# First stage of an attention and two-MLP kernel: exponentials kept unnormalized, rows of values with their sums, normalized on DVE and turned on TensorE

## The chip, the cores and the metric

The kernel runs on one core of one Trainium2 chip. The metric is the device time of one execution in microseconds; three executions were timed before the change. Five engines work side by side, each through its own queue in order: TensorE (PE in the profile, its weight loads PEld), VectorE (DVE), ScalarE (ACT), GpSimd (POOL) and SyncE (SP, which issues DMAs).

## The reference

```
# q, k, v: (2, 8, 768, 64); n_global = 8, n_local = 96
scores = (q @ k^T) / sqrt(64) + bias          # ALiBi: -slope[h] * distance
keep   = (key < n_global) | (0 <= query - key < n_local)
scores = where(keep, scores, -1e9)
a = exp(scores - max)
a = a / (sum(a) + 1e-9)
x = a @ v                                     # 1536 x 512 over both batches
h = elu(x @ w_in);  y = h @ w_out             # 512 -> 2048 -> 512
out = max(y @ w1, y @ w2, y @ w3) @ w_out2    # 512 -> 768 -> 512
```

The weights and inputs are float32 values, the weights passed as 64-bit words that the kernel converts itself.

## The kernel before

Attention is cut into 48 steps: six groups `g` of 256 queries, four pairs of heads `hp`, two blocks `t` of 128 queries. A step takes one block of 128 queries for two heads (`u` = 0, 1). Its keys are a window of 232 columns (96 earlier, 8 global, 128 own); the first block of a batch has only its own 128. I call these wide and narrow steps. In the first group (steps 0 to 7) steps alternate narrow and wide; steps 8 to 15 are wide.

One step runs through these functions: `scores_pe` (two matmuls into PSUM), `scores_dve` (one DVE instruction for each head adds the bias and takes the minimum), `scores_act` (an exponential for each head with the row sum accumulated, which is read out by an instruction of its own), `sums` (ACT adds 1e-9 to the two sums), `recip` and `norm` (DVE: reciprocal, then one multiplication for each head), `turn_pe` (PE turns the probabilities: four transposes of 116 keys, two for a narrow step), `turn_act` (ACT copies the turned tile from PSUM to SBUF), `values_pe` (the values are the stationary operand, the turned probabilities stream past; the result is already turned, head dimension on partitions), `values_high` (ACT rounds it into `xh`) and `values_low` (DVE writes the rest into `xl`).

The first stage is the loop in `windowed`, 18 iterations written out by hand, each engine's order being the order of the calls. Iteration k works on four steps at once: scores, exponentials and sums of step k, normalizing of k-1, turning of k-2, values of k-3. Steps 0 to 15 (the first 512 rows of `x`) are finished there, and steps 16 and 17 begun. The turned tiles cycle through three PSUM banks. From iteration 7 each iteration also takes a piece of the conversion of three weight chunks (`words`), on DVE (`c_low`, `c_word`, `c_rest`) or ACT (`c_rebase`, `c_high`). SP issues the loads in the order of the calls: values (`load_values`, one tile for two steps, each partition 2 KB), queries and keys (`load_pair`), weights (`w_load`). POOL scales the queries (`scale_queries`).

The stage ends with the product `h` of the first weight chunk with `x`: its first half in iterations 16 and 17, the second half at the start of `run`, which goes on with three blocks of 512 rows through the first MLP, the other 32 attention steps between them, and then the second MLP. `run` uses `scores_act`, `norm`, `turn_pe` and `values_pe` in its own order.

Of the kernel before, what the change touches and what calls it, by code (L numbers as in the profile page):

```python
# [12 lines left out]
F32 = mybir.dt.float32  # L13
# [5 lines left out]
ALU = mybir.AluOpType  # L19
PSUM = bass.MemoryType.PSUM  # L20

B, H, S, D = 2, 8, 768, 64
DM, FF, FF2 = 512, 2048, 768
NT = B * S
P = 128
# [9 lines left out]
CH = WIN // 2  # L35
BIG = 1e30
KW = 2 * P + WIN - P + G
GRP = 2 * P
BLOCKS = [512, 512, 512]
# [8 lines left out]
def numbers(nc, pool, n_ap):  # L48

    ni = pool.tile([P, 4], I32, name="ni")  # L50
    nc.sync.dma_start(ni, n_ap.bitcast(I32).partition_broadcast(P))
    w = pool.tile([P, 4], F32, name="nw")
    nc.vector.tensor_copy(w, ni)
    w2 = w.rearrange("p (a b) -> p a b", b=2)
    hi = pool.tile([P, 2], F32, name="nhi")
    nc.vector.scalar_tensor_tensor(
        hi, w2[:, :, 0], 0.0, w2[:, :, 1], op0=ALU.is_lt, op1=ALU.add
    )
    nf = pool.tile([P, 2], F32, name="nf")
    nc.vector.scalar_tensor_tensor(  # L60
        nf, hi, 4294967296.0, w2[:, :, 0], op0=ALU.mult, op1=ALU.add
    )
    return nf[:, 0:1], nf[:, 1:2]


def covered(nc, pool, ng, nl, flag):

    f = pool.tile([P, 4], F32, name="nok")
    nc.vector.tensor_scalar(f[:, 0:1], ng, 0.0, None, op0=ALU.is_ge)
    nc.vector.tensor_scalar(f[:, 1:2], ng, float(G), None, op0=ALU.is_le)  # L70
    nc.vector.tensor_scalar(f[:, 2:3], nl, 1.0, None, op0=ALU.is_ge)
    nc.vector.tensor_scalar(f[:, 3:4], nl, float(PREV + 1), None, op0=ALU.is_le)
    ok = pool.tile([P, 1], F32, name="ok")
    nc.vector.tensor_reduce(ok, f, axis=AX.X, op=ALU.min)
    nc.vector.tensor_copy(flag, ok)
# [33 lines left out]
class Windowed:  # L109
# [4 lines left out]
    def __init__(self, tc, ctx, io, ps, xy, wt, act):  # L114
        self.nc, self.io, self.ps, self.xy, self.wt, self.act = tc.nc, io, ps, xy, wt, act
        self.const = ctx.enter_context(tc.tile_pool(name="acst", bufs=1))
        self.qk = ctx.enter_context(tc.tile_pool(name="qk", bufs=2))
        self.sm = ctx.enter_context(tc.tile_pool(name="sm", bufs=3))
        self.steps = [
            (g, hp, t) for g in range(NT // GRP) for hp in range(HP) for t in range(2)  # L120
        ]
        self.loaded, self.scaled = 0, set()
        self.qk_t, self.v_t = {}, {}
        self.s_t, self.p_t, self.t_t, self.at_t = {}, {}, {}, {}
        self.xraw = {}

    def positions(self, scratch):

# [62 lines left out]
    def load_values(self, k, early=False):  # L191

        if k >= len(self.steps) or k % 2:
            return
        p = k // 2
        pool, tag = (self.act, "gl") if early and p % 2 else (self.qk, "v")
        v = pool.tile([P, 2, 2, P], F32, tag=tag, name="v")
        self.nc.sync.dma_start(
            v.rearrange("p t c f -> p (t c f)"), self.io["v2"][p]
        )  # L200
        self.v_t[k], self.v_t[k + 1] = v[:, 0], v[:, 1]

    def scores_pe(self, k, tags=("S0", "S1"), m=1):
# [50 lines left out]
            m = self.p_t[k][1]  # L254
            self.nc.vector.reciprocal(m[:, 6:8], m[:, 4:6])

    def scores_act(self, k):
        if k >= len(self.steps):
            return
        n = self.geom(k)[-1]  # L260
        p, m = self.p_t[k]
        for u in range(2):
            o = slice(u * WIN, u * WIN + n)
            self.nc.scalar.activation(  # L264
                p[:, o], p[:, o], AF.Exp, bias=m[:, u:u + 1], scale=-1.0,
                accum_out=m[:, 2 + u:3 + u],
            )

    def norm(self, k):
# [37 lines left out]
    def values_pe(self, k, x=None):  # L307
# [5 lines left out]
        for c in range(nch):  # L313
            for u in range(2):
# [3 lines left out]
                    start=c == 0, stop=c == nch - 1,  # L318
                )

    def values_high(self, k, x):

        if k >= 0:
            g, hp, t = self.steps[k]
            o = g * GRP + t * P
            self.nc.scalar.copy(x[0][:, hp, o:o + P], self.t_t[k][0][:, 0:P])

    def values_low(self, k, x):
        if k >= 0:
            g, hp, t = self.steps[k]  # L330
            o = g * GRP + t * P
            self.nc.vector.tensor_tensor(
                x[1][:, hp, o:o + P], self.t_t.pop(k)[0][:, 0:P],
                x[0][:, hp, o:o + P].bitcast(F32), op=ALU.subtract,
            )

# [807 lines left out]
def windowed(tc, ctx, io, flag):  # L1144
    nc = tc.nc
    f = Feed(tc, ctx, io)
    own = ctx.enter_context(ExitStack())
    at = Windowed(tc, own, io, f.ps, f.xy, f.wt, f.act)
    at.close = own.close
    with tc.manual_schedule():  # L1150
        scratch = [f.cv.tile([P, 512], F32, tag="wr", name="sc") for _ in range(2)]
        at.load_pair(0, True)
        f.warm(WARM)
        at.positions(scratch)
        ng, nl = numbers(nc, at.const, io["nn"])
        for p in range(1, 3):
            at.load_pair(p, True)
        at.scale_queries(0)
        at.bases(ng, nl, 0, P + WIN)
        first = BLOCKS[0] // GRP * 8  # L1160
        x = f.split_tiles()

        def convert():
            f.c_rebase(0)
            f.c_low(0)
            yield
            f.c_word(0, 0)
            yield
            f.c_word(0, 1)
            yield  # L1170
            f.c_high(0)
            f.c_rebase(1)
            f.c_low(1)
            yield
            f.c_word(1, 0)
            yield
            f.c_rest(0)
            yield
            f.c_word(1, 1)
            yield  # L1180
            f.c_high(1)
            f.c_rebase(2)
            f.c_low(2)
            yield
            f.c_rest(1)
            yield
            f.c_word(2, 0)
            yield
            f.c_word(2, 1)
            yield  # L1190

        words = convert()
        h = f.ps.tile([P, 512], F32, tag="h", name="h")
        for k in range(first + 2):
            e = k % 2
            at.load_values(k, True)
            if e == 0:
                at.load_pair(k // 2 + 3, k < first)
                at.scale_queries(k // 2 + 1)
            if k <= first:  # L1200
                at.scores_pe(k, (("S0", "S1"), ("y0", "y1"))[e], 1 + (k == first))
            if k >= first:
                f.product(h, f.w[0][:, 0], x, GRP, 0, (k - first) * 6, 6)
            at.values_pe(k - 3)
            at.turn_pe(k - 2, ("TX", "y2", "y3")[k % 3])
            if k < FILL[0]:
                f.fill(at.ident, FILL[1])
            at.scores_dve(k, True)
            at.values_high(k - 3, x)
            at.turn_act(k - 2, nc.scalar.copy)  # L1210
            at.scores_act(k)
            at.sums(k)
            at.recip(k - 1)
            at.norm(k - 1)
            at.values_low(k - 3, x)
            if k >= CONV:
                next(words, None)
            if k in WLOAD:
                f.w_load()
        at.values_pe(first - 1)  # L1220
        at.turn_pe(first, "TX")
        at.values_high(first - 1, x)
        at.turn_act(first, nc.scalar.copy)
        at.values_low(first - 1, x)
        at.recip(first + 1)
        at.norm(first + 1)
        next(words, None)
        f.run(at, first + 2, x, h, lambda: covered(nc, at.const, ng, nl, flag))
# [104 lines left out]
```

## Time and profile before

| what | value |
|---|---|
| median of three executions | 554.83 us (554.69 to 556.24) |
| the profiled execution | 554.8 us, its span 553.0 us |
| busy in the span: PE, DVE, ACT, POOL | 532.5, 394.5, 291.3, 105.1 us |
| mean granted TensorE clock | 0.996 of full speed |

The span goes from the first to the last instruction. Busy time adds up instructions of an engine, overlaps counted once; PE's includes the modelled drain of its passes. In a timeline row the first number is the start, the second the duration, both in us, then engine, line, operation, output and inputs, shapes and count; the brackets hold idle time before it and what ended it. One DVE or ACT instruction can begin a little before the one ahead of it has drained, so the time between two starts is what it costs the queue.

### The profile page before, as it was taken

To read this page: it belongs to the slowest core of one execution; us is meant where nothing else is said; L and a number is where in the kernel's file an instruction comes from. 1 tells how busy PE (TensorE), PEld (TensorE's weight loads), DVE (VectorE), ACT (ScalarE), POOL (GpSimd) and SP (SyncE) were. 2 spreads that over 40 slices of the span, in tenths; PEclk is the share of its full clock that TensorE was granted. 3 is DMA by queue.
4 is the path that set the end of the run, shared out by engine and by line. 5 is a ranking of instruction groups with operands and counts; after the bars stand their busy time and mean duration, and the time that the engine had idled before them with its cause. 6 is when DMAs were issued, how large, how long until landed. Compare 5 with 4: busy or idle time off the path is not lost.

```text
span 553.0 us, 7717 instructions
## 1 busy us (share of the span) xinstructions
PE 532.5 (96%) x2718; PEld 423.2 (77%) x2718; DVE 394.5 (71%) x811; ACT 291.3 (53%) x647; POOL 105.1 (19%) x105
## 2 busy tenths in 40 slices
PE   8889999999999999999999999999999999999995
PEld 6457777767777888887888878878888888888884
DVE  6998999999835444333366747687886979789873
ACT  5998777787846555555355555552147322324120
POOL 4200222222310000000000015431025410335000
PEclk9989999999999999999999999999999999999999
DMA  8919444442201111100000031313008500786024
GB/s 291 393 55 352 159 155 172 140 153 72 91 20 43 29 44 43 38 21 18 0 2 0 1 114 39 114 39 114 1 20 287 208 0 24 241 326 228 2 78 156
DMA packets 23454, 59.20 MB, mean 107 GB/s; under 512 B 2416, under 2 KB 2416, under 8 KB 23408
## 3 DMA queue, kind: packets, MB, share of 16 engines
q1 hardware_dynamic: 18368, 49.46, 25.6%
q10 hardware_dynamic: 5040, 9.18, 4.4%
q8 instruction: 23, 0.38, 0.3%
q14 instruction: 23, 0.19, 0.1%
HBM read 49.19 MB, written 9.44 MB: 106 GB/s over the span
## 4 chain that ended last, share of the span: by engine, by line
PE 72%; DVE 17%; ACT 9%; issue 1%; POOL 0%; ACTq 0%; DVEq 0%; POOLq 0%
PE h L662 19%; PE y L693 11%; DVE wr L457 8%; PE y L937 7%; PE y L701 5%; PE y L1031 4%; PE y L662 4%; PE S L937 4%; ACT w L465 3%; PE S L1031 2%; PE TX L937 2%; DVE p L243 2%; PE S L662 2%; PE TX L293 2%; ACT wr L446 2%; DVE e L687 2%
## 5 line engine op out<-in xcount | busy, mean ns | idle before, releaser
L662 PE MATMUL h<-xh,w 128*128 128x512 f32 (+1 forms) x432 | 115.7, 389 | 0.8 <-ACT xh L642 0.8
L499 POOL TENSOR_TENSOR w<-wr,w 128x512 fp32r<-128x512 f32 x42 | 62.8, 1506 | 232.6 <-ACT w L498 230.4
L693 PE MATMUL y<-gh,w 128*128 128x512 f32 x384 | 98.7, 399 | 0.6 <-ACT gh L669 0.6
L662 PEld LDWEIGHTS h<-xh,w 128*128 128x128 f32 x432 | 79.1, 188 | 19.5 <-issue 1.7
L693 PEld LDWEIGHTS y<-gh,w 128*128 128x128 f32 x384 | 69.6, 188 | 17.1 <-ACT gh L669 1.7
L687 DVE SCALAR_TENSOR_TENSOR e<-e,h 128x512 f32<-128x512 f32 x48 | 32.9, 686 | 54.9 <-ACT e L683 54.9
L662 PE MATMUL h<-xl,w 128*128 128x512 f32 (+1 forms) x216 | 65.9, 386 | 0.0
L498 ACT CAST w<-wr 128x512 fp32r<-128x512 f32 x42 | 27.6, 663 | 63.5 <-DVE wr L489 51.1
L264 ACT ACTIVATE p<-p,m 128x232 f32<-128x232 f32 (+1 forms) x96 | 44.8, 470 | 21.3 <-DVE m L243 21.3
L682 ACT ACTIVATE e<-h 128x512 f32<-128x512 f32 x48 | 28.6, 596 | 50.4 <-PE h L662 45.8
L701 PE MATMUL y<-gl,w 128*128 128x512 f32 x192 | 51.6, 390 | 0.0
L457 DVE SCALAR_TENSOR_TENSOR wr<-wr 128x1024 uint32<-128x1024 uint32 (+1 forms) x36 | 49.9, 1396 | 0.7
L489 DVE SCALAR_TENSOR_TENSOR wr<-wr 128x512 uint32<-128x512 uint32 x48 | 44.2, 922 | 7.5 <-ACT wr L481 6.0
L662 PEld LDWEIGHTS h<-xl,w 128*128 128x128 f32 x216 | 40.3, 188 | 8.3
L669 ACT CAST gh<-e 128x512 fp32r<-128x512 f32 x48 | 29.8, 621 | 30.1 <-DVE e L687 30.1
L937 PE MATMUL y<-t,w 128*128 128x512 f32 x180 | 42.7, 389 | 0.0
L701 PEld LDWEIGHTS y<-gl,w 128*128 128x128 f32 x192 | 36.0, 188 | 8.0 <-issue 0.3
L674 POOL TENSOR_TENSOR gl<-e,gh 128x512 fp32r<-128x512 f32 x16 | 21.0, 1313 | 102.8 <-ACT gh L669 102.8
L937 PEld LDWEIGHTS y<-t,w 128*128 128x128 f32 x180 | 33.8, 188 | 7.0
L674 DVE TENSOR_TENSOR gl<-e,gh 128x512 fp32r<-128x512 f32 x32 | 22.1, 692 | 19.9 <-ACT gh L669 19.9
L187 POOL TENSOR_SCALAR raw<-raw,qsc 128x256 f32<-128x256 f32 x24 | 18.5, 770 | 78.6 <-DMA raw<-qk 78.5
L683 ACT ACTIVATE e<-e 128x512 f32<-128x512 f32 x48 | 30.4, 633 | 1.5
(155 smaller groups left out, 841.9 us busy)
## 6 DMA issues: line engine op xcount, KB each, us to landing
wr<-wa SPq DMA_DIRECT2D x14, 1024.0 KB, 7.1
wr<-wb SPq DMA_DIRECT2D x24, 512.0 KB, 4.5
v<-v SPq DMA_DIRECT2D x24, 256.0 KB, 2.7
part<-row ACTq DMA_DIRECT2D x24, 256.0 KB, 4.2
raw<-qk SPq DMA_DIRECT2D x16, 312.0 KB, 3.8
row<-part SPq DMA_DIRECT2D x12, 256.0 KB, 3.2
out<-rows ACTq DMA_DIRECT2D x11, 256.0 KB, 2.5
raw<-qk SPq DMA_DIRECT2D x8, 260.0 KB, 3.4
```

The lines of the kernel that those rows point to most:

```text
L264: self.nc.scalar.activation(p[:, o], p[:, o], AF.Exp, bias=m[:, u:u + 1], scale=-1.0, accum_out=m[:, 2 + u:3 + u],)
L457: self.nc.vector.scalar_tensor_tensor(r[..., 0], r[..., 1], v, r[..., 0], op0=op, op1=ALU.bitwise_or)
L489: self.nc.vector.scalar_tensor_tensor(t, a, c, t, op0=op, op1=ALU.bitwise_or)
L499: nc.gpsimd.tensor_tensor(w[:, u, 1], v, w[:, u, 0].bitcast(F32), op=ALU.subtract)
L662: nc.tensor.matmul(out[:, o:n], w[:, part % 2, c * P:c * P + P], (xl if part == 2 else xh)[:, c, o:n], start=c == 0 and part == 0, stop=c ...
L674: (engine or self.nc.vector).tensor_tensor(gl[:, 0:n], e[:, 0:n], gh[:, 0:n].bitcast(F32), op=ALU.subtract)
L683: self.nc.scalar.activation(e, e, AF.Exp, scale=-1.0)
L687: self.nc.vector.scalar_tensor_tensor(e, e, -1.0, h, op0=ALU.add, op1=ALU.max)
L693: self.nc.tensor.matmul(y[e][:, 0:n], w[:, a, e * P:e * P + P], g[0][:, 0:n], start=fc == 0 and a == 0, stop=False,)
L701: self.nc.tensor.matmul(y[e][:, 0:n], w[:, 0, e * P:e * P + P], g[1][:, 0:n], start=False, stop=fc == NFC - 1,)
L937: self.nc.tensor.matmul(out, w[:, u, i % 2, b + c * P:b + c * P + P], o[:, i // 2, c], start=c == i == 0, stop=c == 1 and i == 2,)
L1031: nc.tensor.matmul(o, t[:, a, r], w[:, u, b], start=u == k == 0, stop=u == 1 and k == 2,)
```

## The change

In the first stage the exponentials stay unnormalized. `load_values` leaves a column of ones at each end of the 128 value columns (a memset on POOL, and a load in pieces of 512 bytes). `scores_act` drops the accumulated sum for steps below 16. `turn_pe` and `turn_act` come one iteration earlier, on step k-1. `values_rows`, on step k-2, takes the turned exponentials as the stationary operand and streams 65 columns (64 values and the ones) for each head, so that the result has queries on partitions and each head's sum in a column. `rows_norm` (DVE, step k-2) adds 1e-9 to the sums, takes reciprocals and multiplies the rows. `rows_turn` (PE, step k-3) turns the 128x128 result, and `values_high` and `values_low` read it from there. Steps 16 and 17 keep the old way.

```diff
@@ load_values
-        v = pool.tile([P, 2, 2, P], F32, tag=tag, name="v")
-        self.nc.sync.dma_start(
-            v.rearrange("p t c f -> p (t c f)"), self.io["v2"][p]
-        )
+        if k < self.rows:
+            v = pool.tile([P, 2, 2, P + 2], F32, tag=tag, name="v")
+            w = v.rearrange("p t c f -> p (t c) f")
+            self.nc.gpsimd.memset(w[:, :, 0:P + 2:P + 1], 1.0)
+            self.nc.sync.dma_start(
+                w[:, :, 1:P + 1], self.io["v2"][p].rearrange("p (a f) -> p a f", f=P)
+            )
+        else:
...
@@ scores_act
-                accum_out=m[:, 2 + u:3 + u],
+                accum_out=m[:, 2 + u:3 + u] if total else None,
@@ new functions
+    def values_rows(self, k):
...
+        at, v, x = self.at_t.pop(k), self.v_t.pop(k), self.t_t[k][0]
+        kk, nch = (CH, 2) if self.geom(k)[0] else (P, 1)
+        for u in range(2):
+            o = slice(u * (D + 1), (u + 1) * (D + 1))
+            for c in range(nch):
+                a = (nch * u + c) * P
+                self.nc.tensor.matmul(
+                    x[:, o], at[0:kk, a:a + P], v[0:kk, c, o], start=c == 0, stop=c == nch - 1
+                )
+    def rows_norm(self, k):
...
+        nc, x = self.nc, self.t_t[k][0]
+        m = self.sm.tile([P, 8], F32, tag="m", name="r", bufs=4)
+        y = self.y_t[k] = self.sm.tile([P, P], F32, tag="yn", name="yn", bufs=2)
+        nc.vector.tensor_scalar(
+            m[:, 0:2], x[:, 0:2 * D + 2:2 * D + 1], 1e-9, None, op0=ALU.add
+        )
+        nc.vector.reciprocal(m[:, 2:4], m[:, 0:2])
+        nc.vector.tensor_tensor(
+            y.rearrange("p (u d) -> p u d", u=2),
+            x[:, 1:1 + 2 * D].rearrange("p (u d) -> p u d", u=2),
+            m[:, 2:4].unsqueeze(2).to_broadcast([P, 2, D]), op=ALU.mult,
+        )
+    def rows_turn(self, k):
+        if k >= 0:
+            self.nc.tensor.transpose(
+                self.t_t[k][0][:, 2 * P:3 * P], self.y_t.pop(k), self.ident
+            )
@@ loop in windowed
                 at.scores_pe(k, (("S0", "S1"), ("y0", "y1"))[e], 1 + (k == first))
+            at.rows_turn(k - 3)
             if k >= first:
                 f.product(h, f.w[0][:, 0], x, GRP, 0, (k - first) * 6, 6)
-            at.values_pe(k - 3)
-            at.turn_pe(k - 2, ("TX", "y2", "y3")[k % 3])
+            if k <= first:
+                at.turn_pe(k - 1, ("TX", "y2", "y3")[k % 3])
+            at.values_rows(k - 2)
             if k < FILL[0]:
                 f.fill(at.ident, FILL[1])
             at.scores_dve(k, True)
             at.values_high(k - 3, x)
-            at.turn_act(k - 2, nc.scalar.copy)
-            at.scores_act(k)
-            at.sums(k)
-            at.recip(k - 1)
-            at.norm(k - 1)
+            if k <= first:
+                at.turn_act(k - 1, nc.scalar.copy)
+            at.scores_act(k, k >= first)
+            if k >= first:
+                at.sums(k)
             at.values_low(k - 3, x)
+            at.rows_norm(k - 2)
+            if k > first:
+                at.recip(k - 1)
+                at.norm(k - 1)
...
-        at.values_pe(first - 1)
+        at.rows_turn(first - 1)
         at.turn_pe(first, "TX")
```

## Rows read from the trace of the kernel before

**Rows 1.** The page's chain that ended last: shares of the span by engine.
```profile
PE 72%; DVE 17%; ACT 9%; issue 1%; POOL 0%; ACTq 0%; DVEq 0%; POOLq 0%
```

**Rows 2.** Two windows: length; PE, PEld, DVE, ACT, POOL busy (instructions); clock; DMA share; GB/s.
```profile
20.00:25.00 5.00, 3.80 (x34) 2.35 (x36) 4.93 (x15) 4.52 (x17) 0.51 (x2) 1.00 1.04 392
...
30.00:35.00 5.00, 4.92 (x36) 2.97 (x32) 4.93 (x19) 3.73 (x15) 0.00 (x0) 0.72 0.33 116
```

**Rows 3.** Timeline of ACT in one wide step without a conversion.
```profile
34.29 0.49 ACT L264 ACTIVATE p<-p,m 128x232 f32<-128x232 f32 x1
...
34.69 0.19 ACT L264 ACTIVATION_READ_ACCUMULATOR p<-p,m 128x1 f32 x1
34.78 0.47 ACT L264 ACTIVATE p<-p,m 128x232 f32<-128x232 f32 x1
...
35.49 0.25 ACT L326 CAST xh<-y 128x128 fp32r<-128x128 f32 x1
...
35.73 0.59 ACT L304 COPY p<-y 116x512 f32<-116x512 f32 x1
...
36.21 0.49 ACT L264 ACTIVATE p<-p,m 128x232 f32<-128x232 f32 x1
```

**Rows 4.** Timeline: first exponentials of steps 3, 7, 10, 11, 17; the stage's end.
```profile
11.48 0.49 ACT L264 ACTIVATE p<-p,m 128x232 f32<-128x232 f32 x1
...
18.10 0.49 ACT L264 ACTIVATE p<-p,m 128x232 f32<-128x232 f32 x1
...
25.18 0.49 ACT L264 ACTIVATE p<-p,m 128x232 f32<-128x232 f32 x1 [0.54 <-DVE m L243]
...
29.07 0.52 ACT L264 ACTIVATE p<-p,m 128x232 f32<-128x232 f32 x1
...
44.19 0.49 ACT L264 ACTIVATE p<-p,m 128x232 f32<-128x232 f32 x1 [0.16 <-DVE m L243]
...
47.19 0.60 ACT L682 ACTIVATE e<-h 128x512 f32<-128x512 f32 x1 [0.86 <-PE h L662]
```

**Rows 5.** Timeline of DVE in one step with a conversion.
```profile
20.94 1.23 DVE L457 SCALAR_TENSOR_TENSOR wr<-wr 128x1024 uint32<-128x1024 uint32 x1
...
22.07 0.38 DVE L243 CUSTOM_DVE_ANT_0 p<-y,rel 128x232 f32<-128x232 f32 x1
...
22.71 0.15 DVE L255 RECIPROCAL m<-m 128x2 f32<-128x2 f32 x1
...
22.90 0.59 DVE L277 TENSOR_SCALAR p<-p,m 128x232 f32<-128x232 f32 x2
...
23.41 0.29 DVE L332 TENSOR_TENSOR xl<-y,xh 128x128 fp32r<-128x128 f32 x1
...
23.61 1.22 DVE L457 SCALAR_TENSOR_TENSOR wr<-wr 128x1024 uint32<-128x1024 uint32 x1
```

**Rows 6.** Timeline of PE: three and four turning passes, values passes, passes of `h`.
```profile
13.62 0.54 PE L293 MATMUL y<-ident,p 128*116 128x128 f32 x3
13.62 0.65 PE L293 MATMUL y<-ident,p 128*116 128x128 f32 x4
...
36.36 0.66 PE L316 MATMUL y<-p,v 116*64 116x128 f32 x8
...
38.52 0.97 PE L662 MATMUL h<-xh,w 128*128 128x256 f32 x6
```

**Rows 7.** Groups of DVE instructions, 18 to 47.2 us: busy us, mean ns | idle before.
```profile
L332 DVE TENSOR_TENSOR xl<-y,xh 128x128 fp32r<-128x128 f32 x8 | 2.3, 285 | 1.2 <-ACT xh L326 1.2
...
L243 DVE DVE_READ_ACCUMULATOR2_ANT m<- 128x1 f32 x20 | 1.6, 82 | 0.0
```

**Rows 8.** Timeline of loads and POOL: first values issued; queries scaled.
```profile
2.60 0.43 SPq L198 DMA_DIRECT2D v<-v  x1
...
4.02 0.49 POOL L187 TENSOR_SCALAR raw<-raw,qsc 128x256 f32<-128x256 f32 x1
...
13.85 0.48 POOL L187 TENSOR_SCALAR raw<-raw,qsc 128x256 f32<-128x256 f32 x1 [3.51 <-DMA raw<-qk]
```

More of the change, by code (lines that the diff above doesn't have):

```diff
@@ L124, in __init__ @@
         self.s_t, self.p_t, self.t_t, self.at_t = {}, {}, {}, {}
-        self.xraw = {}
+        self.xraw, self.y_t = {}, {}
     def positions(self, scratch):
@@ L196, in load_values @@
         pool, tag = (self.act, "gl") if early and p % 2 else (self.qk, "v")
-        v = pool.tile([P, 2, 2, P], F32, tag=tag, name="v")
-        self.nc.sync.dma_start(
-            v.rearrange("p t c f -> p (t c f)"), self.io["v2"][p]
-        )
+        if k < self.rows:
[6 more added lines that the diff above has]
+        else:
+            v = pool.tile([P, 2, 2, P], F32, tag=tag, name="v")
+            self.nc.sync.dma_start(
+                v.rearrange("p t c f -> p (t c f)"), self.io["v2"][p]
+            )
         self.v_t[k], self.v_t[k + 1] = v[:, 0], v[:, 1]
@@ L255, in recip, with scores_act @@
             self.nc.vector.reciprocal(m[:, 6:8], m[:, 4:6])
-    def scores_act(self, k):
+    def scores_act(self, k, total=True):
         if k >= len(self.steps):
@@ L319, in values_pe @@
                 )
+    def values_rows(self, k):
+        if k < 0:
+            return
+        at, v, x = self.at_t.pop(k), self.v_t.pop(k), self.t_t[k][0]
[8 more added lines that the diff above has]
+    def rows_norm(self, k):
+        if k < 0:
+            return
+        nc, x = self.nc, self.t_t[k][0]
[14 more added lines that the diff above has]
+                self.t_t[k][0][:, 2 * P:3 * P], self.y_t.pop(k), self.ident
+            )
     def values_high(self, k, x):
@@ L325, in values_high @@
             o = g * GRP + t * P
-            self.nc.scalar.copy(x[0][:, hp, o:o + P], self.t_t[k][0][:, 0:P])
+            self.nc.scalar.copy(x[0][:, hp, o:o + P], self.t_t[k][0][:, 2 * P:3 * P])
     def values_low(self, k, x):
@@ L332, in values_low @@
             self.nc.vector.tensor_tensor(
-                x[1][:, hp, o:o + P], self.t_t.pop(k)[0][:, 0:P],
+                x[1][:, hp, o:o + P], self.t_t.pop(k)[0][:, 2 * P:3 * P],
                 x[0][:, hp, o:o + P].bitcast(F32), op=ALU.subtract,
@@ L1159, in windowed @@
         at.bases(ng, nl, 0, P + WIN)
-        first = BLOCKS[0] // GRP * 8
+        first = at.rows = BLOCKS[0] // GRP * 8
         x = f.split_tiles()
```

## The prediction, made before the changed kernel was run

> **What bounds the kernel now.** The chain of work that ended last gives TensorE (PE) most of the span, then DVE and ACT [rows 1]. That share is an average over stages. The change touches one stage, the 18 iterations of the loop in `windowed`, so I read that stage next: its windows, then its timeline. In the windows DVE and ACT are busy up to 4.9 of 5 us, while PE falls to 3.8 [rows 2]; PE's busy time also holds the drain of each pass, so PE is not the bound here.
>
> The timeline shows two kinds of step (I date a step by the start of its first exponential). A step without a weight conversion is ACT's: exponential, read of its sum, exponential, read and `sums`, copy to `xh`, copy of the turned tile, next exponential, back to back, 34.29 to 36.21 = 1.92 us [rows 3]. A step with a conversion on DVE is DVE's: conversion 1.13 (20.94 to 22.07), score passes 0.64, reciprocal 0.19, two normalizing passes 0.51, `xl` 0.20, next conversion at 23.61: 2.67 us [rows 5]. The first eight steps alternate narrow and wide tiles and have no conversion before step 7; steps 3 to 7 take 18.10 - 11.48 = 6.62, or 3.31 a pair [rows 4]. Steps 10 and 14 convert on ACT and are the longest: 25.18 to 29.07, 3.89 us [rows 4]. The stage ends when the product `h` reaches ACT at 47.19, where ACT had stood idle 0.86 [rows 4]; what the stage gains or loses there goes on to the end one for one.
>
> **What the change takes away.** On ACT the read between the exponentials goes (34.69 to 34.78, 0.09), and so do the second read and `sums`: the second exponential, begun at 34.78, needs 0.40 like the first, and the next work began at 35.49, so 0.31. That is 0.40 of 1.92 [rows 3]. On DVE reciprocal and normalizing go, 0.19 + 0.51 = 0.70 [rows 5].
>
> **What it adds on DVE.** `rows_norm` is three instructions, each waiting for the one before: a sum of 128x2, a reciprocal of 128x2, a product of 128x128. The reciprocal today holds its successor for 0.19 [rows 5]; the sum has its shape, so 0.19 each. The product has the shape and the PSUM source of `xl`, 0.285 long [rows 7], of which the queue is held 0.20 [rows 5]. So DVE pays 0.58 for 0.70, and the result is there after 0.19 + 0.19 + 0.29 = 0.67. No row shows a two-column read from PSUM or a scale repeated along a row. Bounds for the 0.67: two instructions as short as DVE's shortest, 0.08, and the product make 0.45 [rows 7]; three as long as a normalizing pass, 0.59 / 2, make 0.89 [rows 5]. I take 0.67, from the nearest shapes.
>
> **What it adds on PE.** Today the values are the weights, 64 columns wide, and the four matmuls of the code show as eight passes in 0.66 us [rows 6]. Afterwards the turned exponentials are the weights, 128 columns wide, and 65 columns of values stream past. The rows bound the spacing of these passes: as today, (0.66 - 0.27) / 7, near 0.055; as in the product `h`, 128-column weights with 256 streamed columns, six in 0.97, near 0.135; the turning passes, 116-column weights with 128 streamed columns, end 0.11 apart (0.54 to 0.65) [rows 6]. What grows is the weights, so I take 0.11. A last pass of 0.27, less half of 0.11 for half the columns, is 0.22: the rows are out after 7 x 0.11 + 0.22 = 0.99. The bounds are 0.6 and 1.17.
>
> [...]
>
> `rows_turn` is one turning pass more, 0.11.
>
> **The order closes a new loop.** PE works in order: scores of k, `rows_turn(k-3)`, `turn_pe(k-1)`, `values_rows(k-2)`. The `rows_turn(k-2)` that follows in the next iteration waits for DVE's `rows_norm(k-2)`, which waits for this iteration's last PE work. Queued behind the waiting `rows_turn` are the next turn and through it ACT's copy and next exponential; only the scores go ahead of it. Before, nothing went from PE to DVE and back within one step. A handover costs about 0.05 (a copy of 0.59 from 35.73 ends at 36.32, the values follow at 36.36) [rows 3, 6]. One wide turn of the loop: four turning passes 0.44, rows 0.99, handover, DVE 0.67, handover, `rows_turn` 0.11 = 2.31, against 1.92. A narrow tile has half the passes: turning a narrow one and making rows of a wide one takes 0.22 + 0.99 + 0.88 = 2.09, the reverse 0.44 + 0.55 + 0.88 = 1.87. A pair is 3.96, against 3.31.
>
> **The sum.** *Up to step 7:* two pairs, 2 x 0.65 = 1.3. Ahead of them the turn and copy of step k-1 now stand between its exponentials and those of k, some 0.6 us where nothing waits at first; part of it is caught up on the narrow steps, and step 3 starts 0.2 late. Together +1.5.
> *Steps 7 to 17.* To step 11: steps 7 and 8 about even, step 9 DVE's with 2.67 - 0.12, step 10 ACT's with -0.40: -0.5. From 11 to 14: `rows_norm` now stands behind `xl`, which waits for ACT's conversion; counted from that conversion's end, DVE reaches the next scores after 0.30 + 0.20 + 0.58 + 1.13 + 0.40 = 2.61, while step 11's exponential starts after 0.72 (`xh` 0.24, copy 0.48); so 1.89, then twice 2.55: 7.0, against 36.21 - 29.07 = 7.14 [rows 3, 4]: -0.1. From 14 to 17: step 14 takes 3.5; the first six passes of `h`, which ran under ACT's conversion at 38.52 [rows 6], are now queued behind the waiting `rows_turn` and ahead of the turn, 6 x 0.135: 1.89 + 0.8; then 2.55. That is 8.7 against 44.19 - 36.21 = 7.98 [rows 3, 4]: +0.7. Together +0.1.
> *The end:* iteration 17 has `rows_norm(15)` besides the old reciprocal and normalizing of step 16, ahead of the last conversion and `xl(15)`, for which `h` waits: +0.6.
> In all about +2.1 us. The profiled execution took 554.8 with its span of 553.0, and the median of the runs is 554.83, so the sum stands for both: 556.9.
>
> **Costed at nothing.** The memsets of the ones columns: POOL idles in this stage, 3.51 us before the tile scaled at 13.85 alone [rows 8]. The loads of values, in pieces of 512 bytes and each behind a memset in POOL's queue, are the third rival; without slack a late one would stop PE at `values_rows`.
>
> **Rivals.** *The loop is short, and the removed work shows* (faster). The place is `values_rows` with `rows_norm`: if together they take under 1.84 - 0.44 - 0.10 - 0.11 = 1.19 (I have 1.66; the lower bounds make 1.05), a wide step is set by exponentials, turn and copy, 0.40 + 0.47 + 0.05 + 0.38 + 0.05 + 0.48, about 1.84, and the first steps come out even. With the short `rows_norm` each of five DVE-bound steps saves 0.12 + 0.22, the two ACT steps 0.40 each, and the end is even: about -2.3, 552.5. For it speaks that the stretch from 30 to 35 us, where the granted clock was 0.72 [rows 2], could be spared as well. Against it: it takes both lower bounds. 12 in 100.
> *The loop costs what the removed work gives* (no change): passes at 0.09, or 0.55 on DVE, take 0.15 us off each of some ten steps: 555.4. 31 in 100.
> *Late values* (slower still). The first load of values was issued at 2.60, with POOL busy up to the queries scaled at 4.02 [rows 8]; behind a memset it goes some 2 us later, and the `raw` and weight loads behind it in SP's queue too. If small pieces halved the rate, eight loads of 0.64 us at some 400 GB/s [rows 2] would add 5 us to a full queue. Against it: the `raw` tile scaled at 13.85 [rows 8] is first used for step 10, whose exponential starts at 25.18 [rows 4]. Were the cover used up, 2 to 3 us more: 559.5. 5 in 100. [...]
> That the change does nothing would need the reads of the sums to stay; nothing speaks for it.
>
> **How the numbers follow.** A measurement of this kernel tells 0.3%, 1.7 us, from no change. The forecast by itself, 556.5 to 558.5, has 52 in 100; with late values slower has 0.57, same 0.31, faster 0.12. Both upper bounds add 0.4 to a wide turn and as much to a pair's halves, and 0.2 to each DVE-bound step: about +5.3, 560.1. The range starts at 553.9, which leaves out the faster rival, and ends at 560.1.
>
> **What would show it.** Right: in steps 3 to 7 PE waits for DVE at `rows_turn` and ACT for PE at the copy; pairs near 4 us; ACT's busy time in the stage falls by some 6 us; `h` reaches ACT near 49.3. Wrong: eight row passes well under 0.9 us, a `rows_norm` under 0.5, ACT without gaps in steps 3 to 7, or PE waiting for a load of values.

## The result and the profile after

The changed kernel takes 563.39 us (five runs, 563.2 to 564.59); the kernel before takes 555.81 beside it (five runs, 554.69 to 556.24). The ratio is 1.0146, with an interval of 1.0129 to 1.0163: slower by 1.5%, 7.6 us, where 2.1 were forecast. The profiled executions stand at 563.39 (span 561.6, granted clock 0.998) and 554.8 (span 553.0), so they lie 8.6 apart; what follows divides up these 8.6. All ratios here compare fast executions alone, and three slow ones of e2 below, near 578 us, are not in its ratio.

**The first stage.** Timeline of ACT in the changed kernel, the first exponentials of steps 3, 7, 11, 14 and 17 (start, length):

```profile
12.44 0.49 ACT L272 ACTIVATE p<-p,m 128x232 f32<-128x232 f32 x1
...
20.65 0.49 ACT L272 ACTIVATE p<-p,m 128x232 f32<-128x232 f32 x1
...
31.49 0.48 ACT L272 ACTIVATE p<-p,m 128x232 f32<-128x232 f32 x1
...
38.64 0.49 ACT L272 ACTIVATE p<-p,m 128x232 f32<-128x232 f32 x1
...
47.23 0.49 ACT L272 ACTIVATE p<-p,m 128x232 f32<-128x232 f32 x1 [0.80 <-DVE m L251]
...
51.03 0.60 ACT L727 ACTIVATE e<-h 128x512 f32<-128x512 f32 x1 [0.78 <-PE h L707]
```

Against [rows 4] the reader sees steps 3 to 7 grow from 6.62 to 8.21 us, steps 11 to 14 stand (7.15 for 7.14), steps 14 to 17 grow from 7.98 to 8.59, and `h` reach ACT at 51.03 in place of 47.19. The stage lost 3.84 us.

In the same windows as [rows 2] DVE falls from 4.93 to 4.31 and PE's granted clock in the second is 1.00 in place of 0.72 (columns as there):

```profile
20.00:25.00 5.00, 4.54 (x38) 3.68 (x37) 4.31 (x19) 4.33 (x11) 1.00 (x3) 1.00 1.05 372
30.00:35.00 5.00, 3.88 (x31) 2.99 (x31) 4.03 (x16) 4.07 (x9) 0.02 (x1) 1.00 0.56 184
```

So the removed work did free DVE, and nobody used it: ACT and DVE wait now. The waits between 10 and 30 us (total, times, longest):

```profile
PEld y L362 <- DVE yn L354: 3.6, 6, 0.7
ACT xh L371 <- PE y L362: 3.1, 6, 0.8
...
DVE r L350 <- PE y L339: 1.9, 4, 0.7
```

L362 is `rows_turn`, L339 the row passes, L350 to L354 `rows_norm`: PE waits for DVE, DVE for PE, and ACT for PE. PE and then DVE in one turn of this loop:

```profile
11.59 0.33 PE L362 MATMUL y<-ident,yn 128*128 128x128 f32 x1 [0.26 <-DVE yn L354]
11.76 0.38 PE L295 MATMUL TX<-ident,p 128*128 128x128 f32 x2
11.97 1.00 PE L339 MATMUL y<-v,p 116*128 116x65 f32 x8
...
13.76 0.33 PE L362 MATMUL y<-ident,yn 128*128 128x128 f32 x1 [0.36 <-DVE yn L354]
```
```profile
13.02 0.16 DVE L350 TENSOR_SCALAR r<-y 128x2 f32<-128x2 f32 x1 [0.47 <-PE y L339]
13.21 0.17 DVE L353 RECIPROCAL r<-r 128x2 f32<-128x2 f32 x1
13.41 0.29 DVE L354 TENSOR_TENSOR yn<-y,r 128x128 f32<-128x128 f32 x1
```

From turn to turn it is 11.59 to 13.76: the turn 0.17, the narrow turning passes 0.21, row passes 1.00, handover 0.05, `rows_norm` 0.68 (13.02 to 13.70), handover 0.06.

**Behind the first stage.** The loss there was to stay as it was. It doubled. Timeline of DVE, the last addition of the whole kernel, before and after:

```profile
547.05 0.69 DVE L1039 TENSOR_TENSOR rows<-y,rows 128x512 f32<-128x512 f32 x1 [0.61 <-PE y L1031]
```
```profile
555.23 0.69 DVE L1084 TENSOR_TENSOR rows<-y,rows 128x512 f32<-128x512 f32 x1 [0.65 <-PE y L1076]
```

8.18 us later, of which 3.84 came with the stage: 4.34 arose in code that the diff doesn't touch (and 0.4 more behind that addition, which makes the 8.6). From the stage's end to this addition the kernel before takes 547.05 - 47.19 = 499.86 us and the changed one 555.23 - 51.03 = 504.20. This "way behind the stage" is the yardstick of the experiments. The groups of PE instructions between 150 and 550 us say where it goes (busy us, mean ns of one pass); before, then after:

```profile
L662 PE MATMUL h<-xl,w 128*128 128x512 f32 x152 | 46.8, 389 | 0.0
...
L701 PE MATMUL y<-gl,w 128*128 128x512 f32 x140 | 37.6, 390 | 0.0
L1031 PE MATMUL y<-w,g 128*128 128x512 f32 x108 | 25.5, 389 | 0.0
```
```profile
L707 PE MATMUL h<-xl,w 128*128 128x512 f32 x156 | 48.5, 392 | 0.0
...
L746 PE MATMUL y<-gl,w 128*128 128x512 f32 x140 | 38.3, 395 | 0.0
...
L1076 PE MATMUL y<-w,g 128*128 128x512 f32 x102 | 24.6, 394 | 0.0
```

The mean pass of these groups, over `xl`, `gl` and `g`, takes 3 to 5 ns more with no wait at all, and PE, which is 96% busy over the whole span, has nothing to hide that behind; the profile has some 1,900 passes in those 400 us, most of them of this length.

What could have changed there is only where tiles lie. The compiled programs' addresses show it: the first stage's odd value tiles borrow the buffers of the tag `gl`. With a column of ones a value tile has 2,080 bytes in a partition in place of 2,048, so the second buffer of `gl` begins 32 bytes later, and the buffers of `gh`, which follow it in the same pool, and all tiles of the pools behind (`xh`, `xl`, `g`) 64 bytes later. The weights, in the pool ahead, stay. In the kernel before all of these tiles lie at the same address modulo 256.

### The profile page after: what moved, and what is told of

The parts are those of the page before. It is cut to its first block, busy times and chain, and to the rows that moved or that the text cites. A ratio compares the mean times of both kernels' runs of the same rounds, so it can differ in the third digit from the quotient of the medians.

```text
span 561.6 us, 7706 instructions
## 1 busy us (share of the span) xinstructions
PE 541.0 (96%) x2734; PEld 431.5 (77%) x2734; DVE 393.8 (70%) x811; ACT 287.2 (51%) x599; POOL 105.6 (19%) x113
## 4 chain that ended last, share of the span: by engine, by line
PE 72%; DVE 15%; ACT 6%; issue 5%; DMA 1%; POOL 0%; SPq 0%; DVEq 0%; POOLq 0%; ACTq 0%
PE h L707 18%; PE y L738 11%; PE y L982 7%; DVE wr L502 7%; PE y L746 6%; PE y L1076 4%; PE y L707 4%; PE S L982 4%; ACT w L510 3%; PE S L1076 2%; PE TX L982 2%; PE S L707 2%; PE h L982 2%; DVE p L251 2%; PE TX L301 2%
## 5 line engine op out<-in xcount | busy, mean ns | idle before, releaser
L543 ACT CAST w<-wr 128x512 fp32r<-128x512 f32 x42 | 27.5, 661 | 63.6 <-DVE wr L534 51.1
L272 ACT ACTIVATE p<-p,m 128x232 f32<-128x232 f32 (+1 forms) x96 | 43.2, 467 | 21.9 <-DVE m L251 21.9
```

Source lines behind the costliest of these rows:

```text
L272: self.nc.scalar.activation(p[:, o], p[:, o], AF.Exp, bias=m[:, u:u + 1], scale=-1.0, accum_out=m[:, 2 + u:3 + u] if total else None,)
```

## The experiments

Two theories for the second half of the loss were set against each other: **addresses** (the longer value tile shifts the operands), and **order** (the changed stage leaves weights and loads in another order, which costs later). For the first half: the **loop** from row passes through `rows_norm` to `rows_turn`, against a plain **start and order** of the steps.

### Addresses

**e1: the kernel before, with the longer tile alone.**

```diff
-        v = pool.tile([P, 2, 2, P], F32, tag=tag, name="v")
+        wide = 520 if early and k < 16 else 512
+        v = pool.tile([P, wide], F32, tag=tag, name="v")
...
+        v = v[:, 0:512].rearrange("p (t c f) -> p t c f", t=2, c=2)
```

> The kernel before with nothing changed but the size of the tiles that hold the values of the first 16 steps: 520 floats a partition as after, of which 512 are used and loaded as before. The first stage should end where it ended before (product h at ACT near 47.2 us). Theory 'addresses' (the wider tile moves the tiles behind it, 64 bytes for the split x and for the second MLP's tiles, and PE's passes over them get a few ns longer): about 4.8 us slower than before, of which 1.0 by the end of the third block and the rest in the second MLP. Rival 'the late loss comes from the changed first stage' (loads, clock, order): within 0.5 us of before.

Its ratio to the kernel before is 1.0086 (1.0047 to 1.0125). The stage ends where it did, and the last addition comes at 551.17:

```profile
46.97 0.60 ACT L682 ACTIVATE e<-h 128x512 f32<-128x512 f32 x1 [0.87 <-PE h L662]
```
```profile
551.17 0.69 DVE L1039 TENSOR_TENSOR rows<-y,rows 128x512 f32<-128x512 f32 x1 [0.66 <-PE y L1031]
```

The way behind the stage is 504.20 us, that of the changed kernel to the hundredth, with the same passes (`xl` 392, `gl` 395, last product 394 ns). The compiled program has the instructions of the kernel before, in the same order; only addresses differ. That settles addresses against order.

**e2: the changed kernel, its odd early value tiles in buffers of another pool, so that the weights, `gh`, `gl`, `xh`, `xl` and `g` have their old addresses** (the second buffer of the other value tiles and the small tiles behind it still lie 32 bytes or more further).

```diff
-        pool, tag = (self.act, "gl") if early and p % 2 else (self.qk, "v")
+        pool, tag = (self.xy, "xy") if early and p % 2 else (self.qk, "v")
```

> The changed kernel with the wide value tiles of odd pairs taken from a pool of larger tiles, so that all later tiles lie where they lay before. Theory 'addresses': the first stage still ends 3.8 us later than before, and the loss stays at 3.8 to the end: about 4.8 us faster than the changed kernel, 558.6. Rival: as the changed kernel, 563.4, with the loss growing from 3.8 to 8 us after the first stage.

Ratio 1.0042 (1.0001 to 1.0082). Passes are back at 389 to 391 ns and the way behind the stage at 500.09. The stage itself ended at 52.88 in the profiled execution, later than in the changed kernel: between 8 and 13 us its PE passes took nearly twice as long (four passes of `z`, a filler product of the first iterations, 1.06 us, 0.61 in the changed kernel). From step 3's exponential, at 14.22, to the end of the stage it took 38.66, as the changed kernel did (38.59).

**e4 and e7: the kernel before with 64 or 128 bytes of padding ahead of the pools of `xh`, `xl` and `g`** (16 or 32 floats, written once by POOL at the start); **e8: the changed kernel, its value tile 2,176 bytes long,** which puts `gl`'s second buffer at +128 and `gh` and the pools behind at +256.

```diff
+        pad = ctx.enter_context(tc.tile_pool(name="pad", bufs=1))
+        self.pad = pad.tile([P, 16], F32, name="pad")
         self.xy = ctx.enter_context(tc.tile_pool(name="xy", bufs=4))
...
+    nc.gpsimd.memset(f.pad, 0.0)
```
```diff
-            v = pool.tile([P, 2, 2, P + 2], F32, tag=tag, name="v")
+            v = pool.tile([P, 2, 2, P + 8], F32, tag=tag, name="v")[:, :, :, 0:P + 2]
```

> The kernel before with 64 bytes of unused space in front of the pool that holds xraw and all pools behind it (and a memset of it on GpSimd at the start); the activation tiles keep their size. Theory 'addresses, by the 64-byte shift': 3 to 4 us slower than before, with mean pass times of h<-xl and of the last product's passes 3 to 5 ns longer, those of y<-gl unchanged. Theory 'addresses, by the 2080-byte activation tile alone': about 1 us or less. Rival 'first stage': no change.

> The kernel before with 128 instead of 64 bytes of unused space in the same place. Theory 'what counts is the start address within 128 bytes': pass times as in the kernel before (389 for h<-xl and for the last product) and no time lost after the first stage. Rival 'any move of these tiles costs': 392 and 394 ns and some 4 us, as with 64 bytes.

> The changed kernel with its value tiles padded from 2080 to 2176 bytes a partition, so that every later tile starts at the same place within 128 bytes as before, though elsewhere. Theory 'start address within 128 bytes': the first stage still ends near 51.0 us, all pass times as before (y<-gl 390, h<-xl 389, last product 389), and about 4 us less than the changed kernel: 559.4. Rival 'any move costs': 563.4.

Ratios: e4 1.014 (1.0055 to 1.0225), e7 1.0161 (1.0075 to 1.0247), e8 1.0073 (1.0047 to 1.01). e4 and e7 also lost in the stage of the profiled execution (its end at 49.33 and 48.01), where the granted clock was low for longer than in the kernel before: 0.50 and 0.64 from 33 to 36 us, where that had 1.00 again. The way behind the stage leaves that out: 504.12 for e4, 505.35 for e7 and 500.37 for e8. The theory that the start within 128 bytes decides fell with e7: its `xl` passes took 395 ns, more than at 64 bytes. With the pools moved by 256 (e8) they are back at 390.

**e9 and e12: is it the operand's own address, or its distance to the weights?** e9 puts 64 bytes ahead of everything, the weights too. e12 puts 64 ahead of the weights and 192 behind them, so that the weights alone move, modulo 256 (the last two lines of the diff are e12's). Both are the kernel before otherwise.

```diff
+        pad = ctx.enter_context(tc.tile_pool(name="pad", bufs=1))
+        self.pad = pad.tile([P, 16], F32, name="pad")
         self.wt = ctx.enter_context(tc.tile_pool(name="wt", bufs=NFC))
+        rest = ctx.enter_context(tc.tile_pool(name="rest", bufs=1))
+        self.rest = rest.tile([P, 48], F32, name="rest")
...
```

> The kernel before with 64 bytes of padding ahead of all of its tiles in SBUF, the weights too, so that operands and weights move together. So far the passes over xl took 389 ns at the old addresses and after a shift of 256 bytes, 392 after 64, 395 after 128, always with the weights where they were. Theory A, what counts is the operand's own start address: the xl passes take 392 ns, those of the last product 394, and gl's, which now move too, more than 390; the last addition starts 3 to 6 us later than 547 with the first stage as before. Theory B, what counts is the distance between operand and weights: all passes stay at 389 to 391 ns and the last addition stays near 547.

> The kernel before with 64 bytes of padding ahead of the weights' pool and 192 behind it: the weights stand 64 bytes further modulo 256, the operands of the passes (xh, xl, gh, gl, g) and all else behind them where they were. When everything moved by 64 together, the xl passes stayed at 389 ns; when all but the weights and the tiles next to them moved, they took 392. Theory (the distance between a pass's operand and its weights counts): xl passes 392 ns or more, y<-gl more than 390, the last product's passes only if its weights lie in that pool; the last addition 2 to 6 us later than 548 for a stage as before. Rival (the distance to another tile behind the weights, such as e or the buffers that ScalarE and VectorE write meanwhile): all stay at 389 to 391 ns and the last addition near 547 to 549.

One run each: e9 556.95 us, e12 562.52 (556.72 for the kernel before beside it). The same groups of PE, 150 to 550 us, of e9 and then of e12:

```profile
L664 PE MATMUL h<-xl,w 128*128 128x512 f32 x152 | 46.8, 389 | 0.0
...
L703 PE MATMUL y<-gl,w 128*128 128x512 f32 x140 | 37.6, 390 | 0.0
L1033 PE MATMUL y<-w,g 128*128 128x512 f32 x108 | 25.5, 389 | 0.0
```
```profile
L666 PE MATMUL h<-xl,w 128*128 128x512 f32 x152 | 47.7, 395 | 0.0
...
L705 PE MATMUL y<-gl,w 128*128 128x512 f32 x140 | 38.4, 396 | 0.0
...
L1035 PE MATMUL y<-w,g 128*128 128x512 f32 x102 | 24.6, 397 | 0.0
```

Everything moved together costs nothing behind the stage (way 500.10); the weights moved alone cost most (507.24). e12 ran on a chip of its own, but its passes over `t`, whose two tiles both lie in the weights' pool, stayed at 389 to 390 ns. So what counted here was how the tiles of these passes lay to the weights, modulo 256 bytes, and not an address by itself: 389 ns for `xl` in e9, 395 in e12.

That each pass goes by the distance of its own two tiles is not shown, and `gl` speaks against it. Its passes come in groups of four, which take its two buffers in turn. In e8 the buffer that moved is the slow one (391 to 394 ns a pass in most of its groups, 389 in those of the other). But in the changed kernel the buffer that stayed where it was is as slow as the one that moved by 32 bytes: here one group of each, the unmoved buffer's from 308.8 to 310.2 us and the moved one's from 314.3 to 315.7:

```profile
L746 PE MATMUL y<-gl,w 128*128 128x512 f32 x4 | 1.1, 396 | 0.0
```
```profile
L746 PE MATMUL y<-gl,w 128*128 128x512 f32 x4 | 1.1, 396 | 0.0
```

From 150 to 550 us the passes of either buffer average 394 ns, one that waited left out. `gh` moved by 64 in the changed kernel and in e1, and by 256 in e8; whether that makes the difference was not tried.

**e10: the changed kernel with that distance kept.** A value tile of 2,304 bytes moves `gl`'s second buffer by 256 and the pools behind by 512.

```diff
-            v = pool.tile([P, 2, 2, P + 2], F32, tag=tag, name="v")
+            v = pool.tile([P, 2, 2, P + 16], F32, tag=tag, name="v")[:, :, :, 0:P + 2]
```

> The changed kernel with its value tile made 256 bytes longer than before the change (2304 bytes, of which 2080 are used), so that gl's second buffer and everything behind it stand at the old addresses modulo 256. Theory (loss = first stage plus address): passes of xl, gl and the last product back at 389 to 391 ns; the loss of the first stage (h at 50.5 to 51.1 where the kernel before has 47.2) is carried to the end almost unchanged, the last addition at 550.6 to 551.3; 559.0 to 559.8, ratio 1.006 to 1.007. Rival (the extra 4 us come from the changed order of work behind the first stage, not from addresses): 563 again.

559.09 us (median of 12; 556.32 for the kernel before), ratio 1.0033 (1.0004 to 1.0063): the time is inside what was expected, the ratio below it (1.006 to 1.007). Passes at 389 to 390 ns, the way behind the stage 499.78. The stage of the profiled execution ended late, at 53.44 in place of 50.5 to 51.1; the granted clock fell twice in it (0.56 to 0.59 from 8 to 12 us, below, and 0.72 from 48 to 51).

These kernels, ordered by the distance of `xl` from the weights (in the last product the roles are exchanged: `g` is what PE loads and the weights `w` stream past):

| kernel | `xl` to weights, bytes mod 256 | `xl` pass, ns | `gl` pass, ns | last product, ns | way behind the stage, us |
|---|---|---|---|---|---|
| before | 0 | 389 | 390 | 389 | 499.86 |
| e9, all moved 64 | 0 | 389 | 390 | 389 | 500.10 |
| e10, pools moved 512 | 0 | 389 | 390 | 389 | 499.78 |
| e8, pools and `gh` moved 256 | 0 (`gl`'s second +128) | 390 | 392 | 389 | 500.37 |
| e4, pools moved 64 | 64 | 392 | 391 | 394 | 504.12 |
| e1 and after | 64 (`gh` too, `gl`'s second +32) | 392 | 395 | 394 | 504.20 |
| e7, pools moved 128 | 128 | 395 | 391 | 395 | 505.35 |
| e12, weights moved 64 | 192 | 395 | 396 | 397 | 507.24 |

### The loop in the first stage

**e5: e2 without the sum of 1e-9 ahead of the reciprocal** (it leaves that addend out; a row's sum is at least 1).

```diff
-        nc.vector.tensor_scalar(
-            m[:, 0:2], x[:, 0:2 * D + 2:2 * D + 1], 1e-9, None, op0=ALU.add
-        )
-        nc.vector.reciprocal(m[:, 2:4], m[:, 0:2])
+        nc.vector.reciprocal(m[:, 2:4], x[:, 0:2 * D + 2:2 * D + 1])
```

> As the changed kernel with the addresses put back, without the instruction that adds 1e-9 to the sums (left out; the sums are 1 or more, so the added amount is lost in float32): rows_norm is a reciprocal and a product. Theory 'loop': each turn of the loop from PE to DVE and back is 0.19 us shorter, so steps 3 to 7 take 7.4 instead of 8.2 us, and the whole stage about 2.4 us less (0.19 in each of 12 to 13 steps, in the others the DVE queue is shorter by as much): product h at ACT near 48.7 us instead of 51.0. Rival 'ACT or the loads set the pace': under 0.5 us.

558.11 us beside 556.17, ratio 1.0015 (0.9977 to 1.0053). Timeline of DVE in e5, `rows_norm`:

```profile
13.34 0.17 DVE L350 RECIPROCAL r<-y 128x2 f32<-128x2 f32 x1 [0.52 <-PE y L339]
13.54 0.29 DVE L351 TENSOR_TENSOR yn<-y,r 128x128 f32<-128x128 f32 x1
```

0.49 in place of 0.68: the loop is 0.19 shorter. From step 3's exponential to `h` at ACT the changed kernel takes 38.59 us and e5 49.21 - 12.76 = 36.45: 2.14 less, about 0.14 a step in some 15 steps (0.51 of it in steps 3 to 7, where 0.8 was expected, 0.59 to step 11, 0.55 to 14, 0.37 to 17). Up to step 7 DVE idles (2.77 us busy of 4 from 16 to 20 in the changed kernel), so a shorter instruction on DVE can help there only through the loop: the loop sets the pace. In the later steps DVE is busy itself (14.04 us of 15.7 from 31.5 to 47.2), and a shorter queue would help as well; which of the two it was there isn't shown. Ahead of step 3, e5 lost some 0.8 us to long passes as in e2 (steps 0 to 3 took 5.62 in place of 4.82), and so did e11 below (5.74).

**e3: the loop to be opened:** e2 with `rows_turn` behind the turning passes, `xh` behind the exponentials and `xl` one iteration later.

```diff
-            at.rows_turn(k - 3)
...
                 at.turn_pe(k - 1, ("TX", "y2", "y3")[k % 3])
+            at.rows_turn(k - 3)
...
-            at.values_low(k - 3, x)
+            at.values_high(k - 3, x)
+            at.values_low(k - 4, x)
...
```

> As the kernel with the addresses put back, with the loop from PE to DVE and back opened: the turn of the normalized rows of k-3 goes behind the turn of k-1, the copy to xh behind the exponentials, and xl one iteration later. Theory 'loop': steps 3 to 7 fall from 8.2 us to about 7 us, PE no longer waits for the normalized rows at the head of an iteration, and the stage ends about 2 us earlier than with the loop: 556.6. Rival 'DVE's sum decides': steps 3 to 7 stay near 8.2 us and the time near 558.6.

593.39 us, ratio 1.0681 (1.0599 to 1.0763): a miss. The edit closed a longer loop. Waits of e3 between 8 and 80 us:

```profile
DVE r L350 <- PE y L339: 23.0, 10, 3.1
ACT p L312 <- PE y L301: 19.5, 7, 4.4
...
PE y L301 <- DVE xl L377: 8.9, 6, 1.8
```

The turning passes need the PSUM tile that `xl` frees, `xl` now stands on DVE behind `rows_norm`, and that waits for PE. PE was busy 6.99 of 10 us from 10 to 20, and from 20 to 70 the granted clock stood at 0.50: a window of ten there (after the busy times come the granted clock, the DMA share and GB/s):

```profile
30.00:40.00 10.00, 6.47 (x30) 5.01 (x28) 5.18 (x18) 3.01 (x8) 0.48 (x1) 0.50 0.55 195
```

It says nothing on the old loop's share.

**e6: only the turn moved:** e2 with `rows_turn` behind the turning passes, and, up to step 7, the copy to `xh` behind that of the turned tile.

```diff
-            at.rows_turn(k - 3)
...
                 at.turn_pe(k - 1, ("TX", "y2", "y3")[k % 3])
+            at.rows_turn(k - 3)
...
-            at.values_high(k - 3, x)
+            if k > 7:
+                at.values_high(k - 3, x)
             if k <= first:
                 at.turn_act(k - 1, nc.scalar.copy)
+            if k <= 7:
+                at.values_high(k - 3, x)
```

> As the changed kernel with the addresses put back, with one move on PE: the turn of the normalized rows of k-3 goes behind the turn of k-1, so that only it and the row passes wait for DVE (and up to step 7 the copy to xh goes behind the copy of the turned tile). Theory 'loop': without the turn the loop is 0.17 + 1.0 + 0.67 + 0.1, near 1.95 us; the step is then set by exponentials, turn, xh and copy, 2.1 and 1.65 us: a pair takes 3.75 instead of 4.1 us, steps 3 to 7 take 7.5; the product h in iteration 16 no longer queues behind DVE; in all 1 to 1.6 us less in the stage. Rival: no change, since ACT waits for PE all the same. Against the opened loop that was run before, xl stays where it was, so no tile is waited for.

566.91 us, ratio 1.0175 (1.0094 to 1.0256). Steps 3 to 7 took 7.82 (12.64 to 20.46) in place of 8.21, so the order is worth 0.4 there (0.7 was expected). Later it cost more than that: in the waits from 32 to 52 us

```profile
ACT xh L371 <- PE y L362: 7.0, 4, 4.6
DVE xl L377 <- ACT xh L371: 3.1, 3, 2.2
```

ACT stands at the turned rows, which are now queued on PE behind turning passes that wait for ACT's own exponentials (1.7 us in the same window). The granted clock was 1.00 from 30 to 33 us, with PE busy 1.87 of 3, and 0.50 from 36 to 51, and the stage ended at 58.42. The way behind it was 500.11.

**e11: the three that helped, together:** e10 without the 1e-9, and with e6's order in steps up to 7 alone (`rows_turn` is issued at its old place where `k > 7`).

```diff
+            if k > 7:
+                at.rows_turn(k - 3)
...
+            if k <= 7:
+                at.rows_turn(k - 3)
```

> As the run before it, and two changes: no 1e-9 is added ahead of the reciprocal (sums are at least 1, so values stay the same in single precision), and in steps up to 7 the turn of the normalized rows goes behind the turn of the exponentials, with the copy of its result behind that of the turned exponentials. Theory (the loop norm, turn, passes sets the pace, and the steps' own order adds to it): steps 3 to 7 take 7.3 us (8.2 in the changed kernel, 7.7 without the addition), the later ones as without the addition, h at 48.8, last addition 549.0, 557.4. Rival (the moved turn only shifts the wait to the copy of the turned values): steps 3 to 7 at 7.7 or more, 557.8 to 558.5. If the granted clock falls in the first stage, as it did with the same order in all steps, 565.

557.79 us (median of 12) beside 556.32, ratio 1.0019 (0.9992 to 1.0046). Steps 3 to 7 took 7.57 (12.89 to 20.46), e5 7.70: with the shorter loop the order gives only 0.13, nearer to the rival, as is the time. The stage ended at 49.26 (e5: 49.21). No version measured here beats the kernel before.

## Why the prediction was half right

**The step that failed** is that the stage's sum "stands for both", the span and the runs, with "what the stage gains or loses there goes on to the end one for one". The carrying itself held: in the changed kernels with the old distances (e2, e3, e5, e6, e10, e11) the way behind the stage is 499.78 to 500.46, within 0.6 of the kernel before, although their stages end between 49.21 and 84.59. But the sum had no term for the longer value tile. It counted what the column of ones costs in instructions and DMA pieces, and not that the tile shares a tag with `gl`. That term is 4.34 us, larger than the stage's whole loss, and e1 makes it without any other edit.

**The stage was mis-sized,** 3.84 for 2.1 (the terms of the forecast as rounded here add up to 2.2):

| part | forecast | profiled | what it was |
|---|---|---|---|
| start (first exponential 7.13 to 7.62) | 0 | +0.49 | the load of `ni`, four integers that DVE waits for, landed 0.3 later; the rest isn't traced. e5 and e11 start at 7.14 and 7.15, so it is no fixed cost of the change |
| steps 0 to 3 | +0.2 | +0.47 | turn and copy between exponentials; that less is caught up on narrow steps is a reading, not tested |
| steps 3 to 7 | +1.3 | +1.59 | pairs of 4.10, not 3.96: the turning passes start 0.16 to 0.17 after `rows_turn`, not 0.11 |
| steps 7 to 11 | -0.5 | -0.13 | step 10 gave 0.39 as forecast; step 8 took 2.12 for 1.83, where I had it even |
| steps 11 to 14 | -0.1 | +0.01 | as forecast |
| steps 14 to 17 | +0.7 | +0.61 | as forecast |
| step 17 to `h` | +0.6 | +0.80 | as forecast |

**The mechanism of the stage was right.** Eight row passes took 1.00 us (0.99 forecast; partly luck, for the first gap was 0.06 and the last pass 0.28, not 0.11 and 0.22), `rows_norm` 0.68 (0.67), the loop with a wide tile's rows 2.17 (2.09). PE waited for DVE at `rows_turn` as foretold; ACT waited for PE more at `xh` (3.4 us from 10 to 30) than at the copy (1.5). ACT's busy time up to the stage's end fell by 4.1 us (37.8 to 33.7), not by some 6. The upper bounds summed to 560.1; the 558.6 to 559.1 that stage and addition make without the address term (554.8 + 3.84, or e10's median) lies inside the range, and the measured 563.39 outside.

From the second of the eight row passes on one started every 0.11 us (12.03, 12.14, 12.26 and on), the spacing that the forecast took from the turning passes.

**The rivals.** The short loop fell with 1.00 and 0.68. That the loop costs only what was removed fell with them for the change as it was made; the kernel comes to lie there once the moved addresses and the addition of 1e-9 are both gone: by their ratios, e5 and e11 are within 0.3% of the kernel before. Late values fell: no wait of PE names a load of values in the waits from 5 to 56 us. The regained clock, which was to speak for the faster rival, did come, 1.00 for 0.72 from 30 to 35 us, and no gain is seen from it: steps 11 to 14, which hold that stretch in the kernel before, took 7.15 in place of 7.14.

What stays open is how the tiles' places lengthen a pass. PE is busy with passes for 96% of the span and with weight loads for 77%, so loads and passes overlap and both read the tiles; no run here separates these reads from those of the other engines. Nor is it shown why the clock fell in the first stage of some profiled executions (0.56 from 10 to 12 us in e10) and not of others (1.00 in the changed kernel).

## What to carry to other kernels

When an edit changes the size of a tile, list what shares its tag and what is allocated behind it, and compare the mean pass of an untouched group before and after: here 3 to 5 ns a pass on the bound engine cost 4.34 us, more than the 3.84 that the edit cost in its own stage. Test it by giving the old kernel the new layout alone; here, padding the tile until everything behind it had moved by multiples of 256 bytes took the loss away (e10: the way behind the stage 499.78 us, 504.20 in the changed kernel). And when freed engines don't make a stage faster, look for a loop between engines inside one step; here an instruction in it cost most of its length in every step, about 0.14 of 0.19 us.

## What was not expected of the hardware

- The mean 512-column pass of these groups took 389 ns or up to 397, by how its tiles lay to the weights modulo 256 bytes. For `xl`: 389 at 0, 392 at 64, 395 at 128 and at 192; for the last product in the same kernels 389, 394, 395 and 397. The price for the whole program was 4 to 7 us of 555 (ways behind the stage of 504.12 to 507.24 us for 499.86). A tile that didn't move was slowed too: the passes over `gl`'s first buffer averaged 394 ns in the changed kernel, 390 for `gl` before.
- The granted clock fell early in one kernel: in e10 PE was busy 0.66 of 2.00 us from 6 to 8, and in the two windows behind it the granted clock was 0.59 and 0.56 (in the changed kernel PE was busy 1.04 of 2.00 us from 6 to 8, and the clock stayed at 1.00):

```profile
8.00:10.00 2.00, 2.00 (x10) 1.42 (x10) 0.23 (x2) 1.24 (x4) 0.56 (x3) 0.59 1.06 412
10.00:12.00 2.00, 2.00 (x12) 1.86 (x12) 0.53 (x5) 0.78 (x2) 0.39 (x1) 0.56 1.05 364
```

- In e2, e5 and e11 passes of nearly twice the length stand beside a granted clock of 1.00 in the record (four passes of `z` 1.06 us; 0.61 in the changed kernel, and 1.04 in e10 beside a granted clock of 0.59), so the column may not show every stretch in which passes take that long.
